# Batch 0 of q and k loaded as 320 and then 256 contiguous tokens, the first part of q on ScalarE's queue

## The chip, the cores and the metric

One Trainium2 chip; the kernel runs on one of its cores. The metric is the device time of one execution in microseconds (us), the median of the runs of a kernel.

## What is computed

The input is q, k, v of shape (4 batches, 8 heads, 576 tokens, 64), all float32. Each head computes two attentions and adds them. One is over tokens averaged in fours (144 averaged tokens) and its result is repeated four times. The other is local: a query sees only keys less than 4 positions away.

```
q_d, k_d, v_d = mean over groups of 4 tokens
out_up    = repeat(softmax(scale q_d k_d^T) v_d, 4)
scores    = where(|i - j| < 4, scale q k^T, -1e9)
out_local = softmax(scores) v
x = (out_up + out_local), as 2304 tokens x 512
h = x @ w_in;  x = (s * relu(h)^2 + b) @ w_out          (512 -> 2048 -> 512)
h = x @ w2_in; out = (h - tanh(h)) @ w2_out             (512 -> 2048 -> 512)
```

## The kernel before, in words

The 2304 tokens are 8 units of 288 tokens (`NB1`); units 0 and 1 are the halves of batch 0. Every matrix product of the two MoE layers is made of float32r matmuls on a high and a low part of each operand. So each weight block (32 of 512 KB for the first layer) is loaded as `wraw` (line 711), cut into its parts by ScalarE, VectorE and GpSimd (lines 724 to 728 and 770 to 778), and then used by TensorE in `l1` (tile `ph`, line 792) and `l2_1` (tile `acc`, line 825). ScalarE applies relu and square to each `ph` (lines 804 to 810).

Batch 0 goes a way of its own, because nothing can start before its attention is done. `b0_load` loads tokens of q or k with the tokens on the partitions (tile `tok`); `b0_tr` transposes them on TensorE into a PSUM tile (`tokT`, line 569) and copies that into `KT` (VectorE, line 577) or, with the factor 1/8, into `QT` (ScalarE, line 573). From `KT` and `QT` come the sums of four tokens (`b0_sum`, line 587), the local scores in blocks of 96 queries and 102 keys (`b0_scores`, tile `S`, lines 599 to 607), their transposes and products with V (`b0_pt`, `b0_pv`, line 624), the averaged attention (`b0_dscores`, `b0_dnorm`, `b0_up`) and the operand x of the first MoE layer (`b0_x`, lines 681 to 689). Between these steps, and so that TensorE's clock stays up, matmuls without use are put in (`warm`, line 910). The PSUM tiles of these steps are taken in turn from a ring of seven places (`RING`, line 67); the same places hold the first `ph` and `acc` tiles of the MoE layer.

Before the change, each partition holds a run of 9 consecutive tokens (64 partitions per head, 2 heads side by side in the partitions). Part 0 of a load is the first 4 tokens of each run and part 1 the other 5, so any contiguous stretch of tokens needs both parts. All these loads are issued on SP's queue, one for 128 partitions.

Two strings write the order down: `LOADS` the loads (K, Q: tensor, pair of heads, part; V; W a weight block) and `ORDER` the steps of unit 0 (k, q: transposes; s: scores; n, p: transposes and products with V; a, b: sums; e, f, u: averaged attention; d: averaged V; w: cut a weight block; x: the operand). `ORDER1` has the steps of unit 1. They set priorities: `pin_order` (line 1661) then has `list_schedule` place every instruction of every engine and queue by modelled times, where what the first 12 MoE matmuls need goes first (`due_times`), and the rest goes in the order of the program. The resulting order is fixed on each engine.

Tile tags `w0` to `w31` are the places of the 32 weight blocks. Until a block is loaded, tokens, V and parts of the attention use some of these places; the second part of q is in `w18` and `w19`.

Of the kernel before, what the change touches and what calls it, by code (L numbers as in the profile page):

```python
# [14 lines left out]
B, H, S, D = 4, 8, 576, 64  # L15
# [45 lines left out]

LOADS = 'K00 K10 Q00 Q10 K01 K11 Q01 Q11 V0 V1 V2 W W W W V3 V4 V5 W W W W W W W W W W W W'
ORDER = 'k00 k10 q00 q10 k01 k11 q01 q11 k02 k12 q02 q12 s00 s01 b01 n00 b23 s10 s20 a0 a1 n10 s11 n01 s21 a2 e0 a3 n20 n11 e1 n21 f0 e2 p00 w d0 f1 e3 p01 d1 u0 p10 w f2 p11 w f3 p20 u1 p21 w x0 x1 w x2'
ORDER1 = 'b01 b23 s30 s31 e0 n31 e1 f0 s40 n30 p30 f1 e2 s41 u0 n40 e3 f2 s51 n41 p31 f3 s50 u1 p40 x3 p41 n50 n51 p50 p51 x4 x5'
RING = '0p1s2ps'
KE = 'DDD'
# [15 lines left out]
def attention_moe_moe_kernel(ctx: ExitStack, tc, q, k, v, w_in, w_out, s_in, b_in, w2_in, w2_out, out):  # L84
    nc = tc.nc
    pe, act, dve, pool, sp = nc.tensor, nc.scalar, nc.vector, nc.gpsimd, nc.sync
# [403 lines left out]


    b0 = {}

    def k_first(j):
        return min(max(QB * j - 3, 0), S - KW)
# [9 lines left out]

    RUN = 9
    PART = ((0, 4), (4, 9))
    CHUNK = ((0, 4), (4, 7), (7, 9))  # L510

    def b0_load(nm, x, part):
        r0, r1 = PART[part]

        n = r1 - r0
        if part:
            t = sb.tile([128, n, 2, D], F32, tag=f"w{16 + 2 * (nm == 'q') + x}", name="tok")
        else:

            if x == 0:  # L520
                b0[nm] = sb.tile([128, 2, n, 2, D], F32, tag=f"w{14 + (nm == 'q')}", name="tok")
            t = b0[nm][:, x]
        for h in range(2):
            a = q if nm == "q" else k
            src = bass.AP(a.tensor, ((4 * h + 2 * x) * S + r0) * D, [[RUN * D, 128], [D, r1 - r0], [1, D]])
            sp.dma_start(out=t[:, :, h], in_=src)
        b0[nm, x, part] = t

    def b0_load_v(j):
# [23 lines left out]
    def b0_ps(shape, u, name):  # L553
        n = ring["n"]
        ring["n"] += 1
        x = RING[n % len(RING)] if u == 0 else "s"
        if x == "p":
            return ps_ph.tile(shape, F32, tag="ph", name=name)
        if x == "s":
            return ps_sd.tile(shape, F32, tag="sd", name=name)  # L560
        return ps_acc.tile(shape, F32, tag=f"acc{x}", name=name)

    def b0_tr(nm, x, c):
        r0, r1 = CHUNK[c]
        part = min(c, 1)
        p_ = b0_ps([128, r1 - r0, 128], 0, "tokT")
        for r in range(r0, r1):
            t = b0[nm, x, part][:, r - PART[part][0]]
            pe.transpose(p_[:, r - r0], t.rearrange("p h d -> p (h d)"), ident)  # L569
        o_ = b0[nm.upper() + "T"].rearrange("p m (g r) -> p m r g", r=RUN)[:, 2 * x:2 * x + 2, r0:r1]  # L570
        i_ = p_.rearrange("p r (a g) -> p a r g", a=2)
        if nm == "q":
            act.activation(out=o_, in_=i_, func=AF.Copy, scale=0.125)
        elif KE[c] == "A":
            act.copy(out=o_, in_=i_)
        else:
            dve.tensor_copy(out=o_, in_=i_)
# [329 lines left out]
    def warm(n):  # L907

        for _ in range(n):
            pe.matmul(warm_t[:, :128], ident, ident, start=True, stop=True)  # L910

    def word(w_, u):
        c, a_ = w_[0], [int(x) for x in w_[1:]]
        if u == 0 and c in WARM_AT:
            warm(WARM)
        if c in "kq":
            warm(3)
        if c == "Q" or c == "K":
            b0_load(c.lower(), *a_)
        elif c == "a" or c == "b":  # L920
            for hq in a_:
                b0_sum("k" if c == "a" else "q", hq, u)
        elif c == "V":
            b0_load_v(*a_)
        elif c == "d":
            b0_vd(*a_)
        elif c == "W":
            w_next()
        elif c == "w":
            w_done()  # L930
        elif c == "q" or c == "k":
            b0_tr(c, *a_)
        else:
            {"s": b0_scores, "n": b0_pt, "p": b0_pv, "e": b0_dscores, "f": b0_dnorm, "u": b0_up, "x": b0_x}[c](*a_, u)

    for w_ in LOADS.split():
        word(w_, 0)
    warm(WARM0)
    for w_ in ORDER.split():
        word(w_, 0)  # L940
# [31 lines left out]
    for u in range(2, NU):  # L972
        c = NF * u
# [725 lines left out]
```

## Time and profile before

| | us |
|---|---|
| three runs | 915.05, 915.94, 922.69 (median 915.94) |
| the profiled execution | 914.84 |
| its span, first to last instruction | 913.1 |
| TensorE's granted clock | full (1.0) over the whole span |

PE is TensorE, PEld its weight loads, DVE VectorE, ACT ScalarE, POOL GpSimd, SP SyncE; a q behind the name is the queue or sequencer of the engine. L569 is line 569 of the kernel before. A row with an arrow reads output<-input. Matmuls overlap, so the busy time of TensorE is not its time at peak.

### The profile page before, as it was taken

What the parts mean: (1) busy time and instruction counts of PE and PEld (TensorE: products, weight loads), DVE (VectorE), ACT (ScalarE), POOL (GpSimd) and SP (SyncE); (2) the same over time, 40 slices, a digit from 0 to 9 for tenths busy, and PEclk for the clock granted to TensorE, in tenths of its full rate; (3) what the DMA queues carried; (4) which work ended last, traced back from release to release, by engine and by line L of the source; (5) the groups of instructions that cost most, each with busy time, mean ns of one, the idle gap of its engine ahead of it and who ended that gap; (6) DMA issues with size and microseconds to landing.
All of it is one profiled execution on the core that took longest, in us unless ns stands there. A gap on an engine that the chain in (4) does not pass through costs nothing.

```text
span 913.1 us, 15490 instructions
## 1 busy us (share of the span) xinstructions
PE 902.2 (99%) x5756; PEld 810.4 (89%) x5756; DVE 697.6 (76%) x1100; ACT 521.0 (57%) x1325; POOL 146.3 (16%) x132
## 2 busy tenths in 40 slices
PE   9999999999999999999999999999999999999998
PEld 8699998999999999999999999888888888888886
DVE  5687999899988989996595889777679547776621
ACT  4999647656676566665686866444336324443321
POOL 1244443422334142231000000000000000000000
PEclk9999999999999999999999999999999999999999
DMA  9970244342142322110397997444354825342151
GB/s 195 396 311 1 83 152 131 116 123 85 55 132 80 107 95 92 39 44 8 111 392 255 389 329 254 126 153 158 120 162 127 284 77 158 115 162 70 47 184 46
DMA packets 81010, 136.20 MB, mean 149 GB/s; under 512 B 23223, under 2 KB 47911, under 8 KB 80935
## 3 DMA queue, kind: packets, MB, share of 16 engines
q1 hardware_dynamic: 79318, 132.86, 43.7%
q10 hardware_dynamic: 1616, 2.36, 0.9%
q8 instruction: 45, 0.74, 0.3%
q14 instruction: 31, 0.25, 0.1%
HBM read 110.48 MB, written 24.71 MB: 148 GB/s over the span
## 4 chain that ended last, share of the span: by engine, by line
PE 91%; ACT 4%; DVE 3%; issue 1%; DMA 0%; POOL 0%; SPq 0%; POOLq 0%; DVEq 0%; ACTq 0%
PE ph L792 23%; PE acc L1058 21%; PE acc L825 20%; PE wb L1197 17%; PE warm L910 2%; PE up L469 2%; PE S L418 1%; PE S L601 1%; ACT wraw L724 1%; PE PT L453 1%; PE O L624 1%; PE xt L318 1%; PE vdps L547 1%; ACT w L775 1%; PE tokT L569 0%
## 5 line engine op out<-in xcount | busy, mean ns | idle before, releaser
L792 PE MATMUL ph<-xh,w 128*128 128x288 f32 x1024 | 231.3, 300 | 2.8 <-DVE gl L813 2.8
L825 PE MATMUL acc<-gh,w 128*128 128x288 f32 (+1 forms) x1024 | 227.9, 298 | 0.9 <-DVE yst L843 0.7
L792 PEld LDWEIGHTS ph<-xh,w 128*128 128x128 f32 x1024 | 171.0, 188 | 8.0 <-DVE gl L813 4.2
L825 PEld LDWEIGHTS acc<-gh,w 128*128 128x128 f32 x1024 | 171.0, 188 | 2.7 <-DVE yst L843 1.2
L792 PE MATMUL ph<-xl,w 128*128 128x288 f32 x512 | 151.9, 297 | 0.0
L825 PE MATMUL acc<-gl,w 128*128 128x288 f32 x512 | 151.2, 296 | 0.0
L1197 PE MATMUL wb<-xoh,w1r 128*128 128x512 f32 x448 | 147.2, 393 | 0.0
L1058 PE MATMUL acc<-w2r,gx 128*128 128x512 f32 x576 | 137.4, 390 | 0.0
L1058 PEld LDWEIGHTS acc<-w2r,gx 128*128 128x128 f32 x576 | 108.1, 188 | 23.3
L1197 PEld LDWEIGHTS wb<-xoh,w1r 128*128 128x128 f32 x448 | 83.9, 187 | 19.9
L792 PEld LDWEIGHTS ph<-xl,w 128*128 128x128 f32 x512 | 96.2, 188 | 0.9 <-issue 0.8
L825 PEld LDWEIGHTS acc<-gl,w 128*128 128x128 f32 x512 | 96.3, 188 | 0.5 <-issue 0.4
L804 ACT ACTIVATE ph<-ph 128x288 f32<-128x288 f32 x128 | 50.7, 397 | 75.7 <-PE ph L792 75.1
L1197 PE MATMUL wb<-xol,w1r 128*128 128x512 f32 x224 | 88.2, 394 | 0.0
L813 DVE TENSOR_TENSOR gl<-ph,gh 128x288 fp32r<-128x288 f32 x128 | 57.5, 450 | 38.9 <-ACT gh L810 38.4
L1191 DVE TENSOR_TENSOR u<-wb,u 128x512 f32<-128x512 f32 x64 | 43.9, 686 | 19.9 <-PE wb L1197 19.8
L267 ACT ACTIVATE pA<-V,a 128x64 f32<-128x64 f32 x198 | 53.6, 340 | 3.4 <-DVE a L256 1.4
L810 ACT CAST gh<-ph 128x288 fp32r<-128x288 f32 x128 | 50.6, 396 | 8.4 <-PE acc L825 5.6
L271 POOL TENSOR_TENSOR pP<-V,a 128x1152 f32<-128x1152 f32 x12 | 33.6, 2804 | 121.0 <-DVE O L279 60.2
L805 ACT ACTIVATE ph<-ph 128x288 f32<-128x288 f32 x128 | 50.9, 397 | 2.3
L1197 PEld LDWEIGHTS wb<-xol,w1r 128*128 128x128 f32 x224 | 42.0, 187 | 9.7
L1183 DVE TENSOR_TENSOR gx<-gT,gx 128x512 fp32r<-128x512 f32 x32 | 22.0, 689 | 36.9 <-ACT gx L1182 36.9
(173 smaller groups left out, 1551.4 us busy)
## 6 DMA issues: line engine op xcount, KB each, us to landing
w2r<-keep_b SPq DMA_DIRECT2D x48, 512.0 KB
wraw<-in_moe_w_in_dram SPq DMA_DIRECT2D x32, 512.0 KB
wraw<-in_moe_w_out_dram SPq DMA_DIRECT2D x32, 512.0 KB
w1f<-keep_a SPq DMA_DIRECT2D x32, 256.0 KB
w1f<-keep_s SPq DMA_DIRECT2D x32, 256.0 KB
keep_b<-w SPq DMA_DIRECT2D x12, 512.0 KB
y<-yst SPq DMA_DIRECT2D x36, 144.0 KB
K<-in_k_dram SPq DMA_DIRECT2D x5, 960.0 KB
```

What stands on the lines that cost most here:

```text
L267: act.activation(out=p_[:, t, h], in_=Vt[u][:, h, o + t], func=AF.Copy, scale=st["a"][:, h * TAU + t, o:o + 1])
L271: eng.tensor_tensor(out=p_, in0=Vt[u][:, :, o:o + TAU, :].rearrange("p h t d -> p t h d"), in1=aw.to_broadcast([128, TAU, 2, D]), op=ALU.mult)
L792: pe.matmul(p_, w_, x_, start=n == 0, stop=n == 3 * KC - 1)
L804: act.activation(out=p_, in_=p_, func=AF.Relu)
L805: act.activation(out=p_, in_=p_, func=AF.Square)
L810: act.copy(out=gh[:, :NB1], in_=p_)
L813: dve.tensor_tensor(out=gl, in0=p_, in1=gh[:, :NB1].bitcast(F32), op=ALU.subtract)
L825: pe.matmul(accs[u][e][:, :g_.shape[1]], w_, g_, start=i == first and n == 0, stop=i == last and n == 2)
L1058: pe.matmul(accs[j][t], g_, x_, start=i == 0 and n == 0, stop=i == NF - 1 and n == 2)
L1183: dve.tensor_tensor(out=t[:, 1], in0=g_, in1=t[:, 0].bitcast(F32), op=ALU.subtract)
L1191: add = lambda o, x, y: dve.tensor_tensor(out=o, in0=x, in1=y, op=ALU.add)
L1197: pe.matmul(b_, w1_op(q_, o, kc, i), xo[x][m][:, kc], start=n == 0, stop=n == 5)
```

## The change

The runs of 9 tokens are gone. Part 0 is now tokens 0 to 319 with 5 consecutive tokens per partition, part 1 tokens 320 to 575 with 4. Each half of the partitions (one head of the pair) is one transfer, so there are 32 transfers of 64 partitions in place of 16 of 128. Part 0 of q is issued on ScalarE's queue. The chunks of the transposes are 3 and 2 tokens of part 0, and 4 of part 1. In `LOADS`, the second part of q goes behind the first four weight blocks and V; in `ORDER`, the second part of k goes behind the first scores, and the transposes of q's second part (q02, q12) to the end.

```diff
-LOADS = 'K00 K10 Q00 Q10 K01 K11 Q01 Q11 V0 V1 V2 W W W W V3 V4 V5 W W W W W W W W W W W W'
-ORDER = 'k00 k10 q00 q10 k01 k11 q01 q11 k02 k12 q02 q12 s00 s01 b01 n00 b23 s10 s20 a0 a1 n10 s11 n01 s21 a2 e0 a3 n20 n11 e1 n21 f0 e2 p00 w d0 f1 e3 p01 d1 u0 p10 w f2 p11 w f3 p20 u1 p21 w x0 x1 w x2'
+LOADS = 'K00 K10 Q00 Q10 K01 K11 V0 V1 V2 W W W W V3 V4 V5 Q01 Q11 W W W W W W W W W W W W'
+ORDER = 'k00 k10 q00 q10 k01 k11 q01 q11 s00 s01 b01 k02 k12 n00 b23 s10 s20 a0 a1 n10 s11 n01 s21 a2 e0 a3 n20 n11 e1 n21 f0 e2 p00 w d0 f1 e3 p01 d1 u0 p10 w f2 p11 w f3 p20 u1 p21 w x0 x1 w x2 q02 q12'
...
+    Q_ENG = [act]
...
-    RUN = 9
-    PART = ((0, 4), (4, 9))
-    CHUNK = ((0, 4), (4, 7), (7, 9))
+    PART = ((0, 5), (320, 4))
+    CHUNK = ((0, 3), (3, 5), (0, 4))
...
+        a, eng = (k, sp) if nm == "k" else (q, sp if part else Q_ENG[0])
         for h in range(2):
-            a = q if nm == "q" else k
-            src = bass.AP(a.tensor, ((4 * h + 2 * x) * S + r0) * D, [[RUN * D, 128], [D, r1 - r0], [1, D]])
-            sp.dma_start(out=t[:, :, h], in_=src)
+            for y in range(2):
+                src = bass.AP(a.tensor, ((4 * h + 2 * x + y) * S + t0) * D, [[n * D, 64], [D, n], [1, D]])
+                eng.dma_start(out=t[64 * y:64 * y + 64, :, h], in_=src)
...
-        o_ = b0[nm.upper() + "T"].rearrange("p m (g r) -> p m r g", r=RUN)[:, 2 * x:2 * x + 2, r0:r1]
+        o_ = b0[nm.upper() + "T"][:, 2 * x:2 * x + 2, t0:t0 + 64 * n].rearrange("p m (g r) -> p m r g", r=n)[:, :, r0:r1]
```

## Rows read from the trace of the kernel before

**Rows 1.** The page, busy time and the chain that ended last, by engine.

```profile
PE 902.2 (99%) x5756; PEld 810.4 (89%) x5756; DVE 697.6 (76%) x1100; ACT 521.0 (57%) x1325; POOL 146.3 (16%) x132
...
PE 91%; ACT 4%; DVE 3%; issue 1%; DMA 0%; POOL 0%; SPq 0%; POOLq 0%; DVEq 0%; ACTq 0%
```

**Rows 2.** Chain in order of time, 0 to 110 us: start us, us, what.

```profile
15.94 1.22 PE S L601 x16
...
26.75 0.14 PE O L624 x2
...
44.11 0.82 PE O L624 x8
...
47.57 0.17 PE xt L681 x2
...
51.19 0.13 PE ph L792
...
53.94 0.40 ACT ph L804
...
79.66 0.60 ACT wraw L724
...
107.09 2.14 PE acc L825 x16
```

**Rows 3.** Windows: stretch, its us, each engine's busy us, PEclk, DMA share, GB/s.

```profile
0.00:5.00 5.00, 3.48 (x16) 3.45 (x17) 0.00 (x0) 1.74 (x3) 4.09 (x34) 1.00 0.54 123
5.00:10.00 5.00, 5.00 (x43) 4.96 (x42) 2.01 (x2) 2.10 (x2) 0.00 (x0) 1.00 1.15 225
10.00:15.00 5.00, 5.00 (x45) 4.92 (x44) 3.73 (x6) 1.22 (x3) 0.00 (x0) 1.00 1.34 210
...
35.00:40.00 5.00, 5.00 (x49) 3.74 (x47) 2.58 (x12) 4.36 (x10) 4.22 (x8) 1.00 1.03 408
40.00:45.00 5.00, 5.00 (x61) 4.57 (x56) 4.15 (x17) 5.00 (x14) 0.26 (x1) 1.00 0.95 371
...
55.00:60.00 5.00, 5.00 (x41) 5.00 (x40) 4.75 (x11) 4.99 (x13) 2.48 (x2) 1.00 1.02 407
60.00:65.00 5.00, 5.00 (x37) 4.64 (x36) 3.86 (x10) 5.00 (x15) 4.97 (x3) 1.00 0.63 246
...
105.00:110.00 5.00, 4.46 (x35) 4.26 (x35) 5.00 (x10) 2.83 (x6) 1.96 (x2) 1.00 0.20 63
```

**Rows 4.** Timeline of SP's queue: start us, us, line, operation, count.

```profile
10.58 7.43 SPq L537 DMA_DIRECT2D vw<-in_v_dram  x6
...
40.42 1.59 SPq L711 DMA_DIRECT2D wraw<-in_moe_w_in_dram  x2
...
50.96 4.17 SPq L711 DMA_DIRECT2D wraw<-in_moe_w_out_dram  x4
```

**Rows 5.** DMA issues by size, loads of k (those of q are alike).

```profile
tok<-in_k_dram SPq DMA_DIRECT2D x4, 160.0 KB
...
tok<-in_k_dram SPq DMA_DIRECT2D x4, 128.0 KB
```

**Rows 6.** Issues on SP (128 KB, 0 to 5 us; 64 KB): ns min/median/max, starts.

```profile
L526 SPq DMA_DIRECT2D tok<-in_k_dram x4: 457/500/507, 0.8 to 2.4; - x4
...
L1083 SPq DMA_DIRECT2D out_dram<-ost x28: 314/420/455, 700.9 to 910.1; - x28
```

**Rows 7.** Timeline of ScalarE (ACT): start us, us, line, operation, idle before.

```profile
7.67 1.10 ACT L573 ACTIVATE QT<-tokT 128x512 f32<-128x512 f32 x1 [5.11 <-PE tokT L569]
...
18.74 1.97 ACT L607 ACTIVATE bs<-S,bnm 96x102 f32<-96x102 f32 x8 [1.97 <-DVE bnm L605]
...
30.04 1.28 ACT L724 ACTIVATE wraw<-wraw 128x512 f32<-128x512 f32 x2
```

**Rows 8.** Timeline 0 to 20 us, TensorE (PE) and VectorE (DVE).

```profile
14.62 0.66 PEld L569 LDWEIGHTS tokT<-ident,tok 128*128 128x128 f32 x5
...
18.13 2.26 DVE L605 TENSOR_REDUCE bnm<-S 96x4 f32<-96x408 f32 x4
```

More of the change, by code (lines that the diff above doesn't have):

```diff
@@ L503, in b0_alloc @@
         b0["kd"] = start.tile([128, 4, G], F32, name="kd")
-    RUN = 9
-    PART = ((0, 4), (4, 9))
-    CHUNK = ((0, 4), (4, 7), (7, 9))
+    PART = ((0, 5), (320, 4))
+    CHUNK = ((0, 3), (3, 5), (0, 4))
     def b0_load(nm, x, part):
-        r0, r1 = PART[part]
-        n = r1 - r0
-        if part:
+        t0, n = PART[part]
+        if part == 0:
             t = sb.tile([128, n, 2, D], F32, tag=f"w{16 + 2 * (nm == 'q') + x}", name="tok")
@@ L564, in b0_tr @@
         r0, r1 = CHUNK[c]
-        part = min(c, 1)
+        part = c // 2
+        t0, n = PART[part]
         p_ = b0_ps([128, r1 - r0, 128], 0, "tokT")
         for r in range(r0, r1):
-            t = b0[nm, x, part][:, r - PART[part][0]]
+            t = b0[nm, x, part][:, r]
             pe.transpose(p_[:, r - r0], t.rearrange("p h d -> p (h d)"), ident)
-        o_ = b0[nm.upper() + "T"].rearrange("p m (g r) -> p m r g", r=RUN)[:, 2 * x:2 * x + 2, r0:r1]
+        o_ = b0[nm.upper() + "T"][:, 2 * x:2 * x + 2, t0:t0 + 64 * n].rearrange("p m (g r) -> p m r g", r=n)[:, :, r0:r1]
         i_ = p_.rearrange("p r (a g) -> p a r g", a=2)
```

## The prediction

> **What bounds the kernel now.** I read the page first (busy time and chain), then the chain in order of time, then busy time by 5 us windows, then the queue of SP and ScalarE's timeline, because the change touches only the first part of the program. TensorE is busy for 902.2 of 913.1 us and carries 91% of the chain [rows 1]: nearly everything after the start is TensorE's own work, which the change doesn't touch. What can change is when that work begins and whether it is fed in its first 50 us. The chain runs over transposes of tokens and scores of batch 0 (S, at 15.94 us), reaches the first matmul of the first MoE layer at 51.19 us, and goes over to ScalarE from 53.94 to 79.66 us; at 107.09 us it is TensorE's for good [rows 2]. So there are two limits in a row: a latency chain up to 51 us, and ScalarE, which is busy for 5.00 of 5 us from 40 to 45 us and for 4.99 from 55 to 60 us [rows 3], busy with weight pieces (wraw, w) and the activations of ph. The time that an earlier start saves reaches the end only if ScalarE comes through its work earlier as well.
>
> Third limit: the DMA engines. They move 123, 225 and 210 GB/s in the first three windows, where the tokens come in 256-byte pieces, and 407 GB/s with a share above 1 from 55 to 60 us, where weights come; in the window 60 to 65 us the share falls to 0.63 [rows 3]: the 32 weights (16.8 MB) are in by some 63 us. The change adds no byte, so that moment hardly moves.
>
> **Part 1, order and size of the first loads.** Today scores wait for all tokens of q and k: 8 transfers of 128 KB and 8 of 160 KB [rows 5], 2.36 MB. By the windows, 0.615 MB are in at 5 us and 1.74 MB at 10 us; 2.36 MB are reached at 10 + 0.62/0.210 = 12.95 us. The last transposes of tokens start at 14.62 us [rows 8], 1.67 us behind their bytes, and S starts at 15.94, 1.3 us behind those. After the change the first unit (tokens 0 to 287 and their neighbours) needs the 320-token part of q and k only: 8 x 160 KB = 1.31 MB. By the same windows: 5 + (1.31 - 0.615)/0.225 = 8.1 us; with the same 1.67 and 1.3 us behind them, S starts at 11.1 us: **4.8 us earlier**. The second part of k (0.52 MB) is in at 10.4 us, and its sums over all tokens at some 14 us, in time for the scores of the averaged attention. V (1.38 MB) follows at some 200 GB/s: in by 17.5 us, before anything asks for it (today the first product with V runs at 26.75 us [rows 2]; 4.8 us earlier is 22). The four weights that the first MoE matmuls need come 0.52/0.2 = 2.6 us earlier, the others at the same time, since the second part of q is only put behind these four.
>
> **Part 2, more and smaller transfers.** 16 transfers of 128 partitions become 32 of 64, so k's first part takes 8 issues instead of 4. An issue on SP costs 0.50 us for 128 KB; the nearest row on a smaller one is 0.42 us for 64 KB stored [rows 6]. I take 0.42. The 8 of k's first part then last 3.4 us on SP instead of 4 x 0.50 = 2.0, but q's first 8 run beside them on ScalarE's queue. Together the two queues offer 160 KB per 0.42 us, more than the 225 GB/s that the DMA engines take, so the engines and not the issue decide; even at 0.50 us each, the last of k's first part is issued at 0.8 + 8 x 0.50 = 4.8 us, well ahead of the 8.1 us at which its bytes are in. SP needs 16 x 0.42 = 6.7 us before V instead of today's 9.8 (V's first issue is at 10.58 [rows 4]). Cost on SP: nothing, bounds -0.5 to +0.6 us on the arrival of the first part. On ScalarE 8 issues of 0.42 us, 3.4 us, stand ahead of its table load and two casts, which then end near 6 us; its next work today is at 7.67 us after 5.11 us of idling [rows 7], so they are covered. Without this cover the evacuations of q would slip by at most the 3.4 us.
>
> Here the Trainium skill speaks against the change. The page "DMA: Bandwidth & Descriptors", section "Rules for kernel authors", advises against two transfers to disjoint partition halves, since they serialize on the same 16 engines, and says that spreading issues over queues saves issue time only. By that rule the 16 added transfers buy nothing and only their issues count; if the four added issues of k's first part stood in the way in full, 4 x 0.42 = 1.7 us would come off the gain and the sum below would be 913.3 instead of 911.6. The windows say that bytes, not issues, set the arrival, and I stay with them.
>
> **Part 3, q's second part goes behind the first unit.** Two evacuations of 4 x 128 columns on ScalarE move from its idle time before 16 us to behind the last x of unit 0. The same form takes 1.10 us [rows 7], so 2.2 us. They now stand in the stretch where ScalarE is full [rows 3]. Between hidden (0) and paid in full (2.2) I take 1.6: full windows from 40 us on, but some 0.6 us of idle before it. The 8 transposes and their waits are on TensorE where it runs warm matmuls; nothing is charged for those. The tiles of q's second part share their places with weights 18 and 19, whose loads are issued at 40.42 us today [rows 4]; they now must wait until those transposes have run. They stand behind PSUM tiles of the last steps of unit 0, the last products with V (from 44.11 us) and the transposes behind them [rows 2]; 4.8 us earlier that is about 40 us, no delay. If not, see the rivals.
>
> **Sum.** ScalarE's first exponential is at 18.74 us, behind a maximum at 18.13 us on VectorE [rows 7, 8]. It moves by 4.8 us with S. The stretch that ScalarE limits moves by the same, less the 1.6 us that it gets to do more: 4.8 - 1.6 = **3.2 us** at 80 us, and TensorE's dense part moves with it. The profiled execution took 914.84 us (span 913.1 and 1.7 around it): 914.84 - 3.2 = **911.6 us**. The median of the three runs, 915.94, lies 1.1 above that execution, so the same sum from the median is 912.7, inside the range. One more thing is open: the order on all engines is worked out anew by the scheduler from modelled times, so stages behind 100 us can come out otherwise. I put that at 2 us to either side, an estimate: four windows like 105 to 110 us, in which TensorE loses 0.54 of 5 us [rows 3].
>
> **The rivals.**
>
> A. *The whole shift comes through.* The evacuations of part 3 fall into gaps, VectorE's sums no longer stand ahead of the maxima (today 2 us between S and the first maximum [rows 2, 8]), so ScalarE gains up to 6 us: 914.8 - 6 = 908.8 us. For it: 5.11 us and more of idle on ScalarE before 18.74 us. Against it: ScalarE can't take weight pieces before they land, and only four come earlier.
>
> B. *Hidden anyway.* The first MoE matmuls start earlier but then wait for weight pieces: DMA is at its rate until 63 us in both kernels, and it saves nothing to be ready before them. Gain 0 to 1.5 us: about 914.5 us. For it: the DMA share above 1. Against it: today's backlog; ScalarE takes its first piece only at 30.04 us [rows 7] and is still on weights at 79.66 us, 16 us after the last one landed, so arrival isn't what it waits for there.
>
> C. *Slower: weights 18 and 19 wait for q.* Should the transposes of q's second part run where they stand in the program, behind the last x of unit 0 (47.7 us today [rows 2]), SP's queue, which is in order, holds weights 18 to 31 from 40.42 until 47.7 us, 7.3 us. The last weights are issued by 55.1 us [rows 4] and land near 63, less 1.7 us of lag: some 6 us of work are in the DMA engines' hands. They run dry for 1.3 us, ScalarE's pieces come that much later, its 2.2 us of evacuations come on top, and as it is then the late weights that feed it, the earlier S buys nothing: 914.8 + 1.3 + 2.2 = 918.3 us. It decides from the point where weight 18 is issued later than 46.4 us. For it: the tiles do share the place. Against it: the scheduler may run the transposes as soon as PSUM has a place.
>
> D. *It doesn't do what it says:* 64-partition transfers move at half the rate, or the two queues share badly, so that the first part is in only at 12 us; S moves by 1 us: 914 us. No row of before shows a 64-partition load. It goes with B in the chances.
>
> **How the numbers follow.** My forecast (909.5 to 913.8) 0.48, A 0.17, B with D 0.24, C 0.11. The range reaches from A's 908.8 less the 2 us of the reordered stages and a little for runs, to C's 918.3: 906.5 to 918.5. A measurement of this kernel tells about 1% (9 us) from no change. Over 1% faster is below 906.8 from the median; only A with luck behind 100 us gets there: 0.06. Over 1% slower is above 925: only C at twice its price, 0.03. Within 1%: 0.91.
>
> **What would show it.** Right: S starts at 11 +- 1 us; the first exponential by 14 us; V's issues begin near 7.5 us; first MoE matmul at 46 to 48 us; weight 18 issued before 43 us; DMA share falls off at 63 us as before; ScalarE leaves the chain at about 77 us. Wrong in part 1: S later than 13 us. Wrong in part 3: first MoE matmul earlier by 4 us or more, and the end by less than 1 us (B), or weight 18 issued behind 46.4 us and a hole in the DMA share between 46 and 55 us (C).

## The result: slower by 1.2%, and the profile after

The changed kernel takes 927.14 us (median of 10 runs, 924.74 to 943.62) against 915.77 us for the kernel before (median of 10): ratio 1.0117, 95% interval 1.0102 to 1.0132. The forecast was 911.6 us, the range ended at 918.5. The profiled execution took 927.04 us, its span is 925.3. In some executions of these and the other kernels here the mean clock was lower (0.97 to 0.98) and the time 15 to 25 us longer; medians of all runs include them, ratios, intervals and means do not.

First the page of the changed kernel: busy time, and the chain that ended last by engine (compare [rows 1]; line numbers are one or two lower than before).

```profile
span 925.3 us, 15520 instructions
...
PE 906.9 (98%) x5756; PEld 812.0 (88%) x5756; DVE 701.3 (76%) x1100; ACT 520.5 (56%) x1325; POOL 148.0 (16%) x132
...
PE 87%; DMA 4%; ACT 3%; DVE 3%; SPq 2%; issue 1%; DVEq 0%; ACTq 0%
```

The span grew by 12.2 us. TensorE idles for 925.3 - 906.9 = 18.4 us in place of 913.1 - 902.2 = 10.9, which is 7.5 us more, and is busy for 4.7 us more with the same 5756 matmuls. The chain now holds DMA with 4% and SP's queue with 2%, which had nothing before. So two things are to be found: what TensorE waited for, and why the same matmuls took longer.

SP's queue after (columns as in [rows 4]):

```profile
0.81 11.87 SPq L524 DMA_DIRECT2D tok<-in_k_dram  x16
12.73 6.40 SPq L535 DMA_DIRECT2D vw<-in_v_dram  x6
19.17 2.33 SPq L710 DMA_DIRECT2D wraw<-in_moe_w_in_dram  x4
21.55 9.54 SPq L524 DMA_DIRECT2D tok<-in_q_dram  x8
31.13 2.02 SPq L710 DMA_DIRECT2D wraw<-in_moe_w_out_dram  x4
...
35.35 3.47 SPq L710 DMA_DIRECT2D wraw<-in_moe_w_out_dram  x3
...
57.26 0.33 SPq L710 DMA_DIRECT2D wraw<-in_moe_w_out_dram  x1
...
59.81 4.17 SPq L710 DMA_DIRECT2D wraw<-in_moe_w_out_dram  x4
```

V is first issued at 12.73 us, where the prediction said 7.5 and the kernel before had 10.58 [rows 4]. Behind the first four weights the eight transfers of q's second part hold the queue from 21.55 to 31.1 us. The last weights are issued from 59.81 us on, before from 50.96. One block of a group of four stands alone at 57.26 us. It is block 15: in the changed kernel its place (tag `w15`, see `b0_load`) holds q's second part, and `w18` and `w19` hold the first, so it can only be loaded when the transposes of the second part have run, which start at 52.05 and 53.05 us.

The loads of tokens one by one (operation, count, ns min/median/max, first and last start in us):

```profile
L524 SPq DMA_DIRECT2D tok<-in_k_dram x16: 534/610/837, 0.8 to 12.1; - x16
L524 ACTq DMA_DIRECT2D tok<-in_q_dram x8: 541/629/648, 0.8 to 6.6; - x8
L524 SPq DMA_DIRECT2D tok<-in_q_dram x8: 533/634/1252, 21.5 to 30.6; - x8
```

A transfer of 64 partitions takes 0.61 us of the queue, 80 KB or 64 KB at a time, more than one of 128 partitions with 128 KB did (0.50 us, [rows 6]) and about as much as one of 128 partitions with 160 KB, from the kernel before:

```profile
L526 SPq DMA_DIRECT2D tok<-in_k_dram x4: 516/560/662, 5.2 to 6.9; - x4
```

And SP waits for landings, as the waits of SP's queue up to 72 us show (line, what it waited for: us in total, times, longest):

```profile
SPq L524 <- DMA wraw<-in_moe_w_in_dram: 3.9, 4, 1.8
...
SPq L524 <- DMA tok<-in_k_dram: 1.3, 3, 0.5
```

In the windows (columns as in [rows 3]) this is what remains of it:

```profile
0.00:5.00 5.00, 3.48 (x18) 3.48 (x19) 0.00 (x0) 0.00 (x0) 4.10 (x34) 1.00 0.49 110
5.00:10.00 5.00, 3.38 (x29) 3.00 (x28) 1.34 (x2) 2.49 (x4) 0.00 (x0) 1.00 0.96 178
10.00:15.00 5.00, 5.00 (x43) 4.29 (x41) 3.15 (x7) 1.82 (x3) 0.00 (x0) 1.00 0.49 111
...
50.00:55.00 5.00, 4.04 (x33) 3.65 (x31) 3.77 (x9) 2.34 (x5) 0.00 (x0) 1.00 0.96 388
55.00:60.00 5.00, 3.36 (x31) 2.99 (x32) 2.04 (x5) 5.00 (x11) 3.33 (x9) 1.00 1.03 412
...
65.00:70.00 5.00, 5.00 (x38) 4.64 (x37) 4.46 (x8) 5.00 (x14) 3.13 (x2) 1.00 1.01 400
70.00:75.00 5.00, 4.24 (x34) 3.68 (x33) 2.87 (x11) 5.00 (x15) 1.43 (x2) 1.00 0.25 102
...
160.00:165.00 5.00, 3.10 (x25) 2.54 (x24) 5.00 (x4) 3.64 (x15) 2.79 (x4) 1.00 0.04 12
165.00:170.00 5.00, 5.00 (x20) 4.10 (x19) 1.78 (x3) 1.10 (x3) 0.78 (x2) 0.50 0.34 100
170.00:175.00 5.00, 5.00 (x35) 4.60 (x35) 4.00 (x7) 2.27 (x11) 1.38 (x2) 0.82 0.16 56
```

The share of the DMA engines is 0.49 from 10 to 15 us (before 1.34 [rows 3]). They are busy with weights until 71 us, where before the share fell to 0.63 in the window from 60 to 65. TensorE loses 0.96 and 1.64 us between 50 and 60 us. Far later, behind a window with 3.10 us of work, its granted clock is 0.50 and then 0.82: a stretch at 1.2 instead of 2.4 GHz, which costs (1 - 0.50) x 5 + (1 - 0.82) x 5 = 3.4 us, most of the 4.7 us by which the same matmuls are longer. Before, the clock was full everywhere.

The stall at 54 us stands in ScalarE's timeline (start us, us, line, operation, in brackets the idle time before and what ended it), and below it in TensorE's:

```profile
53.38 0.70 ACT L723 ACTIVATE wraw<-wraw 128x512 f32<-128x512 f32 x1 [2.09 <-DMA wraw<-in_moe_w_in_dram]
54.64 0.65 ACT L723 ACTIVATE wraw<-wraw 128x512 f32<-128x512 f32 x1 [0.56 <-DMA wraw<-in_moe_w_in_dram]
55.20 0.39 ACT L803 ACTIVATE ph<-ph 128x288 f32<-128x288 f32 x1
55.53 1.99 ACT L572 ACTIVATE QT<-tokT 128x512 f32<-128x512 f32 x2
```

```profile
53.41 0.63 PE L598 MATMUL S<-bandr,identr 96*96 96x408 f32 x2
56.64 0.60 PE L600 MATMUL S<-KT,QT 64*96 64x102 f32 x8 [2.61 <-ACT QT L572]
```

ScalarE waits for weights that land late, and the evacuation of q's second part is queued behind them in its fixed order; TensorE waits 2.61 us for that evacuation.

Counting matmuls shows where the time is lost. The first `ph` matmul is 1.5 us early (49.5 us, before 51.0), but the first `acc` matmul is 5.6 us late (62.0, before 56.4). The 257th `acc` is 7.5 us late (156.7, before 149.2), the 385th 13.0 (206.2, before 193.2), the end 12.2.

This reads like a finished story: slow issues, late weights, a blocked evacuation, a clock that fell. The first seven runs were made to divide it up, and they didn't add up. The eleventh showed why.

### The profile page after: what moved, and what is told of

It reads as the page before. It is cut to its first block, busy times and chain, and to the rows that moved or that the text cites. A ratio compares the mean times of both kernels' runs of the same rounds, so it can differ in the third digit from the quotient of the medians.

```text
span 925.3 us, 15520 instructions
## 1 busy us (share of the span) xinstructions
PE 906.9 (98%) x5756; PEld 812.0 (88%) x5756; DVE 701.3 (76%) x1100; ACT 520.5 (56%) x1325; POOL 148.0 (16%) x132
## 4 chain that ended last, share of the span: by engine, by line
PE 87%; DMA 4%; ACT 3%; DVE 3%; SPq 2%; issue 1%; DVEq 0%; ACTq 0%
PE ph L791 23%; PE acc L1057 21%; PE acc L824 20%; PE wb L1196 17%; DMA wraw<-in_moe_w_in_dram 3%; PE up L469 2%; PE S L418 1%; SPq L524 1%; SPq L535 1%; PE xt L318 1%; PE PT L453 1%; ACT wraw L723 1%; SPq L710 1%; DMA tok<-in_k_dram 0%; DVE ppqk L392 0%
```

## Experiments

Medians are of 4 runs, or 5 (e14). "Ratio" is to the kernel before, run on the same chip alongside. In the first seven expectations the theory *count* says that the queue time of the transfers decides when V and the weights come; their theory *order* means the order of the loads and steps in the two strings `LOADS` and `ORDER`. In the last two groups *order* means what the scheduler makes of it on all engines.

### The transfers alone, and the strings alone

e2, the kernel before with each load in two transfers:

```diff
-            src = bass.AP(a.tensor, ((4 * h + 2 * x) * S + r0) * D, [[RUN * D, 128], [D, r1 - r0], [1, D]])
-            sp.dma_start(out=t[:, :, h], in_=src)
+            for y in range(2):
+                src = bass.AP(a.tensor, ((4 * h + 2 * x + y) * S + r0) * D, [[RUN * D, 64], [D, r1 - r0], [1, D]])
+                sp.dma_start(out=t[64 * y:64 * y + 64, :, h], in_=src)
```

> The kernel before, with each load of tokens cut into two transfers of 64 partitions (32 in all, all on SP); runs of 9 tokens, order and everything else as before. Theory count (a transfer of 64 partitions occupies its queue for about 0.61 us, so the number of transfers, not their bytes, sets when V and the weights start): 32 x 0.61 = 19.5 us of issues instead of 9.8, V's first issue near 20 us instead of 10.6, last weights in some 8 us later, 922 to 926 us. Theory order (what costs is that q's second part is loaded and evacuated late): nothing of the order is changed, 914 to 917 us.

932.95 us, ratio 1.0161 (1.0086 to 1.0236). The 32 issues last from 0.81 to 22.7 us on SP's queue, at 0.62 us each:

```profile
L527 SPq DMA_DIRECT2D tok<-in_k_dram x16: 611/619/752, 0.8 to 16.2; - x16
L527 SPq DMA_DIRECT2D tok<-in_q_dram x16: 614/617/1195, 6.2 to 22.0; - x16
```

e3, the changed kernel with `LOADS` and `ORDER` of the kernel before (the first four lines of the change's diff, undone):

> The kernel after, with the two strings of the order (LOADS and ORDER) of before: q's second part loaded ahead of V and transposed ahead of the scores; still 320 and 256 tokens in halves, first part of q on ScalarE's queue. Theory count: 24 issues on SP ahead of V, 24 x 0.61 = 14.6 us, V's first issue near 15.5 us, but no small transfers stand between weights: 917 to 922 us. Theory order: 914 to 917 us.

932.0 us, ratio 1.0136 (1.0060 to 1.0212). Both above their expected ranges.

e6, the kernel before with each load cut along the tokens, so that 32 transfers keep 128 partitions:

```diff
-            src = bass.AP(a.tensor, ((4 * h + 2 * x) * S + r0) * D, [[RUN * D, 128], [D, r1 - r0], [1, D]])
-            sp.dma_start(out=t[:, :, h], in_=src)
+            m = (n + 1) // 2
+            for c0, c1 in ((0, m), (m, n)):
+                src = bass.AP(a.tensor, ((4 * h + 2 * x) * S + r0 + c0) * D, [[RUN * D, 128], [D, c1 - c0], [1, D]])
+                sp.dma_start(out=t[:, c0:c1, h], in_=src)
```

> The kernel before, with each load of tokens cut in two along its tokens (2 + 2 and 3 + 2 of each run) instead of along its partitions: 32 transfers of 128 partitions, all on SP. Theory count (any further transfer costs about 0.6 us of SP's queue): 32 issues last 20 us as in the kernel cut by partitions, V's first issue near 21 to 23 us, 928 to 935 us. Rival, partitions (a transfer is dear because it covers only 64 partitions; with 128 an issue of half the bytes costs about 0.42 us): 32 x 0.42 = 13.4 us, V's first issue near 14.5 us, 917 to 921 us.

924.69 us, ratio 1.0094 (1.0076 to 1.0113), between the two. Its issues:

```profile
L528 SPq DMA_DIRECT2D tok<-in_k_dram x16: 453/468/487, 0.8 to 17.9; - x16
L528 SPq DMA_DIRECT2D tok<-in_q_dram x16: 467/469/1532, 2.8 to 16.9; - x16
```

This much is settled: at the same number of bytes and of transfers, an issue takes 0.47 us with 128 partitions (e6) and 0.62 with 64 (e2). The same tokens hold SP's queue for 9.7 us in 16 transfers (before), for 17.5 in e6's 32 and for 21.9 in e2's 32. So the number of transfers and their partitions count. The bytes aren't without effect: with 128 partitions the issue takes 0.47 us for 64 to 96 KB, 0.50 for 128 KB and 0.52 to 0.66 for k's 160 KB; the last of these also stand later in the queue, and no run separates the two.

### Which queue

e4: all of q on SP (`Q_ENG = [sp]`). e5: all of q on ScalarE. e7: the second parts of k and q on GpSimd. e8: the kernel before with only the first part of q on ScalarE's queue. In this order:

```diff
-    Q_ENG = [act]
+    Q_ENG = [sp]
...
-        a, eng = (k, sp) if nm == "k" else (q, sp if part else Q_ENG[0])
+        a, eng = (k, sp) if nm == "k" else (q, Q_ENG[0])
...
-        a, eng = (k, sp) if nm == "k" else (q, sp if part else Q_ENG[0])
+        a, eng = (k if nm == "k" else q), pool if part else (sp if nm == "k" else act)
...
-    nc = _bacc.Bacc("TRN2", target_bir_lowering=False, num_devices=1, dynamic_dma_scratch_size=256)
+    nc = _bacc.Bacc("TRN2", target_bir_lowering=False, num_devices=1, dynamic_dma_scratch_size=384)
...
-            sp.dma_start(out=t[:, :, h], in_=src)
+            (act if nm == "q" and not part else sp).dma_start(out=t[:, :, h], in_=src)
```

> The kernel after, with the first part of q issued on SP too. Theory count: 24 issues ahead of V on one queue, V's first issue near 15.5 us instead of 12.7, 928 to 932 us. Theory order: the order is that of after, 925 to 928 us.

> The kernel after, with the second part of q issued on ScalarE's queue as well, right behind the first, so that no small transfer stands between weights on SP. Theory count: SP has 16 small issues, V as in after (12.7 us), the weights follow without the break from 21.5 to 31 us, last weights in at some 65 us instead of 71; less what 8 issues (5 us) on ScalarE ahead of q's evacuations cost: 917 to 921 us. Theory order: the steps of q's second part stand as late as in after, 923 to 927 us.

> The kernel after, with the second parts of k and q issued on GpSimd's queue (its descriptor scratch raised from 256 to 384 bytes): SP has only the 8 issues of k's first part ahead of V, and no small transfer between weights. Theory count (SP's issue time and its places for transfers under way set when the weights come): V's first issue near 6.2 us, first weight near 12 us instead of 19, last weights in by 61 to 64 us instead of 71, 909 to 915 us: the gain that was forecast comes back. Theory order (q's second part is evacuated late and blocks ScalarE and TensorE near 55 us): 921 to 927 us. Against the first: GpSimd's own issues may be dear or late, then k's sums are late.

> The kernel before with one thing of the change: the first part of q (4 transfers of 128 partitions) issued on ScalarE's queue. Theory count: SP has 12 instead of 16 issues ahead of V, V starts 2 us earlier; DMA engines then limit: 912 to 916 us. Rival, a second queue harms (its packets interleave with k's, so the first piece of k comes later): 917 us or more.

| | us | ratio |
|---|---|---|
| e4 | 940.13 | 1.0229 (1.0154 to 1.0304) |
| e5 | 943.42 | 1.0266 (1.0163 to 1.0369) |
| e7 | 963.42 | 1.0529 (1.0507 to 1.0551) |
| e8 | 920.51 | 1.0056 (1.0038 to 1.0074) |

The first three lie 8 us or more above both of their ranges. In e4, V is first issued at 16.66 us, near the 15.5 that theory count named, but its time is far above; what costs it the rest wasn't traced. Of e5, TensorE's windows show why a queue that also has work to do is no free queue: ScalarE's queue holds eight more transfers ahead of the first evacuation, which starts at 14.17 us (changed kernel: 8.83), and TensorE has nothing to do in the window from 10 to 15 us. Its clock falls.

```profile
5.00:10.00 5.00, 3.27 (x28) 2.89 (x26) 1.33 (x2) 1.74 (x3) 0.00 (x0) 1.00 0.98 177
10.00:15.00 5.00, 0.00 (x0) 0.00 (x0) 0.00 (x0) 0.83 (x1) 0.00 (x0) 0.67 0.79 176
```

Of e7, GpSimd's timeline shows issues of 0.62 us that start some 6 us apart, so that k's last transfer is issued at 37.94 us:

```profile
31.54 0.62 POOL L524 DMA_DIRECT2D tok<-in_k_dram  x1 [5.50 <-issue]
37.94 0.62 POOL L524 DMA_DIRECT2D tok<-in_k_dram  x1 [5.77 <-issue]
```

The trace has the landings, too: GpSimd's transfers go one at a time. The one issued at 31.54 us lands at 37.63, and the next is issued 0.3 us later; so it is with all eight of k. Whether the engine or the size of the descriptor scratch sets this was not tried.

e8 was the puzzle: no transfer is added, the first weight is issued at 17.57 us (before, V's issues end at 18.01 [rows 4]), and yet it is 0.6% slower. Its time lies in the range of its rival, but not for the rival's reason: k's first piece doesn't come later, S starts at 15.72 us (before 15.87 in the same view).

### The order that the scheduler makes, and the control

The order on every engine comes from `list_schedule`, which reckons 450 ns for each issue. e9 tells it 640 ns for a transfer of 64 partitions. e10 names q's second part eight weights later. e11 names the transposes of q's second part earlier. In this order:

```diff
+ISSUE64 = 640.0
...
-        return ISSUE, 0.0
+        p = list(w.ap)[0][1]
+        return (ISSUE64 if p == 64 else ISSUE), 0.0
...
-LOADS = 'K00 K10 Q00 Q10 K01 K11 V0 V1 V2 W W W W V3 V4 V5 Q01 Q11 W W W W W W W W W W W W'
+LOADS = 'K00 K10 Q00 Q10 K01 K11 V0 V1 V2 W W W W V3 V4 V5 W W W W W W W W Q01 Q11 W W W W'
...
-ORDER = 'k00 k10 q00 q10 k01 k11 q01 q11 s00 s01 b01 k02 k12 n00 b23 s10 s20 a0 a1 n10 s11 n01 s21 a2 e0 a3 n20 n11 e1 n21 f0 e2 p00 w d0 f1 e3 p01 d1 u0 p10 w f2 p11 w f3 p20 u1 p21 w x0 x1 w x2 q02 q12'
+ORDER = 'k00 k10 q00 q10 k01 k11 q01 q11 s00 s01 b01 k02 k12 n00 b23 s10 s20 a0 a1 n10 s11 n01 s21 a2 e0 a3 n20 n11 e1 n21 f0 e2 p00 w d0 f1 e3 p01 d1 u0 p10 w f2 p11 w f3 p20 u1 p21 w q02 q12 x0 x1 w x2'
```

e12 is the control: the kernel **before**, with one constant of the scheduler's model changed.

```diff
-SLACK = 300.0
+SLACK = 360.0
```

> The changed kernel, its transfers unchanged, but the scheduler, which places the work of every engine by 450 ns for an issue, is told 640 ns for an issue of 64 partitions, about what the trace shows (0.61 to 0.66 us). SP's first 16 issues stay at 11.9 us and V's first at 12.7 us. If the late weights themselves are the loss (theory queue time), the time stays at 923 to 929 us. If the loss is made by an order worked out for earlier arrivals, with a Prelu that waits for a late weight standing ahead of the evacuation of q's second part on ScalarE (theory order), TensorE's stall of 2.6 us at 54 to 57 us goes, the half clock at 160 us goes with the stalls ahead of it, and the time is 916 to 920 us.

> The changed kernel with the second part of q named eight weights later in the list of loads; the scheduler then puts half of its eight transfers ahead of weight 4 and half ahead of weight 8. If the break of 9.5 us in the weight issues between 21.5 and 31 us is a loss by itself, half of it moves to a later place and weight 4 is issued some 4 us earlier: 922 to 925 us. If the eight transfers cost the same wherever they stand among the weights, since the queue waits for landings anyway, 926 to 929 us.

> The changed kernel with the transposes of q's second part named ahead of the last steps of unit 0 (x0) and not at the very end; no transfer is changed. If the 2.6 us that TensorE waits for the evacuation QT at 54 to 57 us comes through to the end, and the half clock at 160 us follows from what is late there, the time is 919 to 924 us. If the weights, which come in 8 us later than before, are what everything waits for, the stall only moves to another instruction and the time stays at 925 to 929 us.

> The kernel before with one constant of the scheduler's model changed (360 ns instead of 300 allowed for a hand-over between engines): no instruction and no transfer is added or changed, only the order on the engines from the first MoE matmuls on. It measures what a new order alone does. The prediction allowed 2 us to either side: 913 to 918 us. If new orders by themselves make up most of the loss, it comes out 5 to 10 us from the kernel before, 920 us or more.

| | us | ratio |
|---|---|---|
| e9 | 924.31 | 1.0094 (1.0077 to 1.0111) |
| e10 | 927.52 | 1.0146 (1.0111 to 1.0181) |
| e11 | 921.11 | 1.0067 (1.0052 to 1.0082) |
| e12 | 926.23 | 1.0112 (1.0095 to 1.0129) |

Of the two ranges that each of them names, e9 fell into the first, e10 into the second and e11 into the first. In e9 and e11 TensorE no longer waits for QT (it is busy for all 5 us from 55 to 60 us in both), yet one gains 2.8 us and the other 6.0, so the stall alone doesn't set the time. e12 is the test: the same work on every engine, the same transfers, and it is as slow as the changed kernel. Its SP queue up to the first weights is that of the kernel before ([rows 4]):

```profile
10.44 7.36 SPq L537 DMA_DIRECT2D vw<-in_v_dram  x6
17.84 2.44 SPq L711 DMA_DIRECT2D wraw<-in_moe_w_in_dram  x4
```

The page's busy time is not ([rows 1]):

```profile
span 924.4 us, 15495 instructions
...
PE 911.2 (99%) x5756; PEld 816.2 (88%) x5756; DVE 700.9 (76%) x1100; ACT 518.3 (56%) x1325; POOL 150.9 (16%) x132
```

Nor are the windows from 50 us on ([rows 3]):

```profile
50.00:55.00 5.00, 4.23 (x31) 3.14 (x29) 4.10 (x8) 5.00 (x14) 2.82 (x3) 1.00 1.02 410
55.00:60.00 5.00, 3.91 (x15) 3.45 (x15) 3.51 (x6) 3.31 (x9) 0.62 (x1) 0.52 1.03 409
60.00:65.00 5.00, 5.00 (x23) 4.81 (x22) 3.05 (x6) 2.98 (x10) 1.48 (x2) 0.50 0.55 219
65.00:70.00 5.00, 5.00 (x35) 4.65 (x35) 3.24 (x7) 4.65 (x16) 2.38 (x2) 0.96 0.02 3
```

Of the 11.3 us by which its span is longer, TensorE idles for 924.4 - 911.2 - 10.9 = 2.3 us and is busy for 9.0 us longer; the clock from 55 to 70 us takes 2.4 + 2.5 + 0.2 = 5.1 of these, and the other 3.9 were not traced. The kernel before has 5.00 us of work and a full clock in its window from 55 to 60 us [rows 3].

### Both kernels with orders that nobody chose

e13, e14 and e19 are the kernel before with 240, 330 and 400 ns; e17, e15 and e16 the changed kernel with 240, 330 and 360; e18 is e11 with 360.

> The kernel before with 240 ns allowed for a hand-over between engines in the scheduler's model in place of 300: the same instructions and transfers in another order. If orders spread widely and the kernel before has a good one (theory order), 920 to 928 us, as the 926.2 us with 360 ns; if 360 ns was an unlucky value and orders mostly lie close together (theory transfers), 913 to 918 us.

> The kernel before with 330 ns in place of 300, again only another order. Theory order: 920 to 928 us. Theory transfers: 913 to 918 us.

> The changed kernel with 330 ns in place of 300: its transfers as they are, another order. If the transfers (issues of 0.61 to 0.66 us, weights in by 71 us instead of 63) cost 8 us or more whatever the order, it stays some 8 us above the kernel before with the same 330 ns: 925 to 936 us where that one has 917 to 928. If the order is what costs, the two kernels with 330 ns lie within 3 us of each other.

> The changed kernel with 360 ns, beside the 926.2 us of the kernel before with 360 ns. If the transfers cost 8 us or more by themselves: 934 us or more. If the order is what costs and each new order is a new draw: 918 to 930 us, on either side of 926.2.

> The changed kernel with 240 ns, a third pair beside the 925.0 us of the kernel before with 240 ns. Theory order (the two sets of transfers are worth the same, and 300 ns was a good value for the kernel before alone): 920 to 929 us. Theory transfers (they cost 8 us or more): 932 us or more.

> The changed kernel with the transposes of q's second part ahead of x0 (921.1 us with 300 ns) and with 360 ns, where the changed kernel took 922.0. If what the two edits do adds up: 916 us. If each is a new draw of an order: anywhere from 918 to 929 us. A version below 914 us would beat the kernel before.

> The kernel before with 400 ns, a fourth new order. Theory order: 920 to 929 us, so that no new order of five comes near the 915.7 of the kernel before. If it lies below 918 us, the order of before isn't rare, and the spread alone explains less.

| constant, ns | kernel before, us (ratio) | changed kernel, us (ratio) |
|---|---|---|
| 240 | 924.95 (1.0097) | 923.80 and 925.78 |
| 300, as given | 915.7 | 927.14 (1.0117) |
| 330 | 928.40 (1.0137) | 927.17 (1.0116) |
| 360 | 926.23 (1.0112) | 922.04 (1.0076) |
| 400 | 925.33 (1.0105) | |

Of e17, whose median is 933.85 us, the table has the two executions that the means use. e13, e16, e17 and e19 lie in the range of their theory order, e14 0.4 us above it, and e15 within 3 us of e14, as that theory said. e18 missed both of its ranges: it took 930.37 us, ratio 1.0162 (1.0140 to 1.0184): two edits that gave 921.1 and 922.0 alone give 930.4 together.

So no new order of the kernel before comes nearer than 9 us to its own, and at 240, 330 and 360 ns the two kernels lie within 5 us of each other. By the means the changed kernel differs by +0.3 (924.8 against 924.5), -1.8 (926.2, 928.0) and -3.0 us (922.6, 925.6), -1.5 in the mean. Three such pairs tell this neither from nothing nor from the 3.2 us that was predicted; they exclude that the transfers cost some 8 us or more whatever the order. With the pair at 300 ns, +11.4, the mean of four is +1.7; but there the kernel before has its own order, the one that no other comes near.

The clearest single row against the story of the late weights is e16's. Its transfers and SP queue are those of the changed kernel, its weights come as late:

```profile
55.00:60.00 5.00, 5.00 (x44) 4.17 (x41) 3.71 (x7) 5.00 (x13) 4.21 (x10) 1.00 1.02 410
...
65.00:70.00 5.00, 5.00 (x40) 5.00 (x39) 5.00 (x9) 5.00 (x15) 2.58 (x2) 1.00 1.01 401
```

The DMA share is above 1 until 70 us here too, yet TensorE has 5.00 us of work in the window from 55 to 60 us, where the changed kernel has 3.36. And e13, the kernel before with 240 ns, has its weights on time (0.55 in the window from 60 to 65) and loses 6.8 us of clock, 5.1 of them between 25 and 40 us and 1.7 between 55 and 65. The first fall:

```profile
20.00:25.00 5.00, 5.00 (x36) 3.73 (x34) 1.62 (x5) 4.06 (x17) 0.00 (x0) 1.00 0.97 342
25.00:30.00 5.00, 5.00 (x27) 4.33 (x28) 2.26 (x9) 2.38 (x8) 0.00 (x0) 0.53 1.03 418
30.00:35.00 5.00, 5.00 (x8) 1.11 (x6) 2.31 (x8) 4.61 (x13) 0.75 (x1) 0.50 1.01 391
```

What the seven runs of the first two groups say must be read against this spread. Kernels that differ from one of the two in their order alone have ratios from 1.007 (e11) to 1.016 (e18). e6 lies inside that and e2 and e3 at its upper end, with intervals that reach far beyond it, so their times decide nothing on transfers; only their issue durations do. e4, e5 and e7 lie outside; for e5 and e7 the rows above show a stage that starves. e8 lies below, better than any new order of the kernel before, so q's first loads on ScalarE's queue may be worth a few us; with one order alone that isn't shown. No version beat the kernel before.

## Why the prediction was wrong

**The step that failed is the last term of the sum**, "stages behind 100 us can come out otherwise. I put that at 2 us to either side". Measured on the kernel before, with nothing else touched, it is 9 to 13 us, and to one side: four new orders of four are slower. The estimate was made from four windows in which TensorE idles a little. It left out that the profiled order was one order, with no row on how others would do. And it left out the clock: in every profiled execution here but that of the kernel before, TensorE has stretches at 1.2 GHz, at a price of 1.7 us (e16), 3.4 (changed kernel), 5.1 (e12) and 6.8 (e13).

The clock is not the whole price. The spans of these four are 7.2, 12.2, 11.3 and 10.8 us longer than before, so 4 to 9 us of each are something else. One execution of e9 kept the full clock (mean 1.000) and took 925.15 us, one of e6 922.37: 9.5 and 6.9 us above the kernel before (both have more transfers, too). What else a new order loses, and whether the order of before was picked or was luck, stays open.

"Behind 100 us" was wrong too: e13's clock falls at 25 us, e12's at 55, and the first `acc` matmul of the changed kernel is late at 62. Nor is the chain TensorE's "for good" from 107.09 us on: in the kernel before it leaves TensorE again at 144.85 us for 1.92 us of VectorE. "TensorE's dense part moves with it" rested on that reading.

**Part 1** was right in direction. S starts at 12.9 us, 3.0 earlier than before and not 4.8; the first exponential at 15.35 us (before 18.74), not 14. The first MoE matmul starts at 49.5 instead of 46 to 48 us (before 51.0):

```profile
12.92 0.59 PE L600 MATMUL S<-KT,QT 64*96 64x102 f32 x6
...
15.35 1.04 ACT L606 ACTIVATE bs<-S,bnm 96x102 f32<-96x102 f32 x4 [2.01 <-DVE bnm L604]
...
49.47 0.38 PE L791 MATMUL ph<-xh,w 128*128 128x288 f32 x1
```

Of the 1.8 us by which S is later than forecast, 1.2 are the bytes: at 110 and 178 GB/s in the first two windows, where the forecast used 123 and 225, 1.31 MB are in at 9.3 us and not at 8.1. Of the 4.8 us, 1.5 were left where the MoE layer begins.

**Part 2** was wrong in its own term. "I take 0.42" was the stored 64 KB; the loads of 64 partitions measure 0.61, and nearer rows had said 0.50. The last transfer of k's first part is issued at 6.90 us, not by 4.8, as three of its issues waited for landings (1.3 us). The 16 issues of k last 11.9 us instead of 6.7. That "the engines and not the issue decide" may hold up to 10 us (share 0.96), but from 10 to 15 us the share is 0.49 with the weights unissued and V just begun: there the issue decides. That V comes 2.2 us later than before and the last weights some 8 is thus shown, and it is the transfers' doing. That it costs the time is not: e16 has both and takes 922.0 us.

The Trainium skill, "DMA: Bandwidth & Descriptors", section "Rules for kernel authors", had advised one transfer of 128 partitions over two halves, since the halves share the same engines. The runs add a cost on the queue: 2 x 0.61 us of issue against 0.50 to 0.66. The 913.3 us worked out by that rule misses for the same reason as the sum.

**Part 3** had the evacuations at 2.2 us, measured 1.99. What it didn't see is that on ScalarE a fixed order can put them behind a weight that isn't there yet; 2.61 us on TensorE. e11 takes that away and gains 6 us, but as e18 shows, such gains can't be told from a lucky order. It also had the wrong place: q's second part was in `w18` and `w19` before the change and is in `w15` after it, and its transposes run at 52 us, not at 40.

**The rivals.** C named the right side by a mechanism that did not occur. SP doesn't wait for the transposes of q's second part: weight 18 is issued at 45.42 us, later than the forecast's 43 and ahead of C's 46.4, and the one block that has to wait, 15, was placed behind eleven others. B's picture, ScalarE waiting for weight pieces, is in the trace (2.09 and 0.56 us), though B forecast it as a lost gain and not as a loss. D gave 914, with transfers at half the rate; in the window from 5 to 10 us they moved 178 GB/s instead of 225. The 0.49 after it comes from the queue, which had only k's second part to issue.

## What to carry to other kernels

Where a scheduler fixes the order of all engines from modelled times, the kernel before is one order out of many, perhaps a picked one (this is not shown): any edit throws it away. Change a constant of the model in the kernel before, measure that spread first (here 9 to 13 us), and put it into the forecast and behind every experiment before rows are read as causes. For the first loads, count issues as well as bytes: more and smaller transfers are paid on the queue that the later loads stand in.

## What was not expected of the hardware

- At equal bytes an issue of 64 partitions takes longer than one of 128: 0.62 us (e2) against 0.47 (e6). SP and ScalarE agree (0.61 and 0.63 in the changed kernel). With 128 partitions 160 KB took up to 0.66 us for k.
- Issues of GpSimd take 0.62 us and start up to 6.4 us apart, each about 0.3 us after the transfer ahead has landed (e7).
- The granted clock falls to 0.50 in some orders and not in others. The window ahead of the fall shows 3.10 us of work in one case, 4.23 in another (e12) and 5.00 in a third (e13); the longest idle time of TensorE just ahead of it is 0.99, 0.95 and 0 us. The profile's busy time didn't foretell the fall, and what does was not settled.
